# A first MoE layer with fp16 operand pairs, TensorE in order of emission, and attention over 14 of 16 chunks

## The chip, the core and the metric

The program runs on one core of one Trainium2 chip. The metric is the device time of one execution in microseconds (us), of which the median of several executions counts.

## The reference, cut to what matters

Attention over 4 batches, 8 heads, 576 positions and 64 columns a head (causal mask, and a bias that falls with the running sum of `max(s, 0)`), then two MoE layers of 2304 tokens, 512 model columns and 2048 features:

```python
attn = softmax(scores)                       # scores from q, k, the mask and cumsum(max(s, 0))
x = (attn @ v) as (2304 tokens, 512)
h = x @ w_in;  g = h * tanh(log1p(exp(h)));       x = g @ w_out      # first MoE
h = x @ w_in2; g = h / (1 + exp(-1.702 * h));     out = g @ w_out2   # second MoE
```

q, k, v and s come as float32, the four weights as float64.

## The kernel before, in words

**Numbers in pairs.** Nearly every product is made of operands that are split in a high and a low part, and of three matmuls: high by high, high by low, low by high (`mm3`, L814). In the first layer of the first MoE the parts are of type fp32r (32 bits), in the second MoE of fp16. The float64 weights are read as pairs of 32-bit words and joined on the chip: a Prelu on ScalarE, a shift and an or on VectorE; then a copy on ScalarE gives the high part and a subtraction on GpSimd the low part (`turn_w` L764; written apart as `turn_words`, `turn_join`, `turn_parts` at L793 to L812 for the first five weights).

**The stages.** (1) A prologue whose order is written out by hand (L868 to L944, mode "strict": each engine takes its instructions in the order of the program text). It loads, does the first six steps of attention, turns the first five of the 16 blocks of `w_in` and multiplies dummies (`warm`). (2) From there to the end of attention, `first_layer` (L968) makes h = x @ w_in for the first seven of nine spans of U = 256 tokens, in 16 chunks a span (one block of 128 features, 12 matmuls each). After every chunk `slot_a` (L962) runs as many attention steps (`tick`, L678) as the span owes. A tick emits the scores of step t (`do_qk`), their minimum on VectorE (`do_max`), the exponential on ScalarE (`do_exp`), the split in fp16 parts and their transposing DMA (`do_hilo`), the preparation of later groups of heads (`pop_prep`), and the product with v of the step LAG ticks back (`do_av`, `emit_tile`). Batch 0 has 26 steps of another form: its probabilities are transposed by TensorE and copied out by VectorE (`early_pt`), and its steps lag by 2. The other 78 steps use the DMA. (3) The last two spans (L1073 to L1088, 384 matmuls into accumulators named acc), while the 16 blocks of `w_out` are turned. (4) The second layer of the first MoE, and (5) the second MoE, both to the end of the program.

**What sets the order.** A scheduler with its own estimate of time orders each engine's instructions when the program is built. `Line` and `Lane` (L56 to L89) tie instructions to the one before: "strict" in the prologue; "after" from there to step 26, the first of batch 1 (NEAR), where an instruction is only kept behind the prologue's last; no tie from step 26 on (L690).

**Weights and buffers.** Twelve raw blocks of `w_in` are asked for at the start, on SyncE's queue (UP); a further one is asked for after a turned block (`bg_a`, L834). The pool wa has 16 buffers of 4 KB a partition, for raw blocks and for turned ones. The chunks' results go through the pool mo_a (MA = 5 buffers) to DRAM, written by SyncE's queue, and so do the loads of v for its scale (`vscale_load`, L312). Transposing DMAs stand on SyncE's queue too.

Of the kernel before, what the change touches and what calls it, by code (L numbers as in the profile page):

```python
# [18 lines left out]
PSC = 32768.0  # L19
VTOP = 16384.0  # L20
PH = 3
# [4 lines left out]
MA = 5  # L26
MBB = 2
# [4 lines left out]
HLB = 3  # L32
PB = 2
XTB = 2
PTB = 5
WAH = 3
NP0 = 5
FROM = 7
# [5 lines left out]
UQ = 2  # L44
WTOP = 8192.0
# [6 lines left out]
LAG = 4  # L52


class Line:
# [4 lines left out]
    def __init__(self, nc, tie):  # L60
        self.nc, self.tie, self.mode, self.last = nc, tie, None, {}
# [7 lines left out]
class Lane:  # L69
# [3 lines left out]
    def __getattr__(self, op):  # L73
# [4 lines left out]
        def run(*a, **kw):  # L78
# [14 lines left out]
def attention_moe_moe_kernel(  # L93
# [81 lines left out]


# [131 lines left out]

    vsc, vmx = {}, {}
# [14 lines left out]
    def vscale_set(b):  # L324
# [11 lines left out]
        nc.vector.tensor_scalar(out=t[:, 1:2], in0=t[:, 0:1], scalar1=PSC, scalar2=None, op0=ALU.mult)  # L336
# [273 lines left out]
    def norm_tile(x):  # L610
# [4 lines left out]
        nc.vector.tensor_scalar(out=rs, in0=su, scalar1=1e-9, scalar2=vsc[x["b"]][:, 1:2], op0=ALU.add, op1=ALU.mult)  # L615
        nc.vector.reciprocal(rs, rs)
        nc.gpsimd.tensor_tensor(out=ts["x"], in0=ts["x"], in1=rs.to_broadcast([128, nu, D]), op=ALU.mult)

    def emit_tile(x):
        b, i, n = x["b"], x["i"], x["n"]  # L620
# [6 lines left out]
        pv = ps[:, 0:KC * n].rearrange("p (c t) -> p c t", c=KC)  # L627
        t0 = b * S + 128 * i
        done = 0
        while done < n:  # L630
            u, off = divmod(t0 + done, U)
            m = min(n - done, U - off)
            if u not in xunit:
                xunit[u] = xh_a.tile([128, 2, KC, U], F32R, tag="xh", name="xh")
# [3 lines left out]
            nc.scalar.activation(out=hi, in_=src, func=AF.Copy)  # L638
            nc.vector.tensor_tensor(out=xu[:, 1, :, off:off + m], in0=src, in1=hi, op=ALU.subtract)
# [10 lines left out]
    def queue_prep(gi):  # L650
# [13 lines left out]
        items = items + vs  # L664
        if b + 1 < B and (i, g) in VSTEP:
# [14 lines left out]
    def tick():  # L680
        t = nxt[0]
        nxt[0] += 1
        if t < NS:
# [6 lines left out]
            if t >= NEAR:  # L690
                nc.mode = None
# [41 lines left out]
    I32 = mybir.dt.int32  # L733
# [30 lines left out]
    def turn_w(pool, lay, m, kind):  # L764
        t = pool.tile([128, 2, DM], F32R, tag="w", name="w")
        (win_t if kind == "in" else wout_t)[lay, m] = t
        r = fetched.pop((lay, m, kind))
        th, tl_ = t[:, 0, :], t[:, 1, :]
        if not wide:
            nc.scalar.activation(out=th, in_=r, func=AF.Copy)  # L770
            nc.vector.tensor_tensor(out=tl_, in0=r, in1=th, op=ALU.subtract)
            return
# [699 lines left out]
```

## Time and profile before

| what | us |
|---|---|
| three executions | 999.42, 1004.05, 1008.64 |
| median | 1004.05 |
| the profiled execution | 1001.29 |
| its span, first to last instruction | 999.3 |

The profile is of one execution: 2.0 us of its 1001.29 lie outside the span. PE is TensorE's matmuls, PEld its loading of weights, DVE VectorE, ACT ScalarE, POOL GpSimd, SP SyncE (SPq: a queue's own entries). All instructions carry line L79, that of the helper that records them, so they are told apart by the names of what they write and read: h<-xh,w is the first layer in its first seven spans, acc<-xh,w in its last two, h<-x,w2i the first layer of the second MoE, wst a raw block of weights, pt the transposed probabilities.

### The profile page before, as it was taken

The numbers are of one execution on the slowest core, as the hardware profiler recorded it, in microseconds if no ns is written. First come the engines' busy times: TensorE is split into PE (matmuls) and PEld (weight loads), VectorE is DVE, ScalarE is ACT, GpSimd is POOL, SyncE is SP. The second block draws the span as 40 slices with busy tenths as digits, with TensorE's granted clock in tenths as the row PEclk, the third lists the DMA queues.
The fourth block names the chain that finished last, engine by engine and source line by source line (L and its number), as shares of the span: only waits on it lengthen the run. The fifth ranks groups of instructions, "written<-read, shape, count | busy, mean of one in ns | idle before, by whom it ended". The sixth has DMA issues, their size and how long they took to land.

```text
span 999.3 us, 20234 instructions
## 1 busy us (share of the span) xinstructions
PE 968.8 (97%) x7974; PEld 863.0 (86%) x7974; DVE 676.8 (68%) x1363; ACT 554.3 (55%) x1062; POOL 289.1 (29%) x358
## 2 busy tenths in 40 slices
PE   8989998989999999999999999999999999999997
PEld 6868996979889889998888888888888888888886
DVE  6878677774666874788997967985554654653553
ACT  5656577785667874786565845643333433333331
POOL 5636442442144330000000000054342424333341
PEclk9999999999999999999999999999999999999999
DMA  9931688996689977899995653400100100000000
GB/s 257 342 88 40 186 192 166 178 239 149 157 167 223 191 144 188 308 330 357 380 308 181 233 187 107 127 1 16 49 22 1 44 23 1 22 22 1 22 13 32
DMA packets 157262, 142.26 MB, mean 142 GB/s; under 512 B 90000, under 2 KB 126352, under 8 KB 157168
## 3 DMA queue, kind: packets, MB, share of 16 engines
q1 hardware_dynamic: 150240, 122.22, 43.9%
q0 software_dynamic: 6928, 18.75, 6.9%
q8 instruction: 63, 1.03, 0.4%
q14 instruction: 31, 0.25, 0.1%
HBM read 89.09 MB, written 32.58 MB: 122 GB/s over the span
## 4 chain that ended last, share of the span: by engine, by line
PE 83%; DMA 5%; DVE 4%; issue 2%; ACT 1%; POOL 0%; SPq 0%; DVEq 0%; POOLq 0%; ACTq 0%
PE h L79 31%; PE acc L79 25%; PE p L79 16%; PE s L79 5%; PE o L79 3%; DMA pt<-hl 3%; PE kt L79 1%; PE qt L79 1%; DMA qraw<-in_q_dram 1%; PE pt L79 1%; DMA vraw<-in_v_dram 1%; DVE w2l L79 1%; PE xt L79 0%; DVE P L79 0%; DMA vl<-in_v_dram 0%
## 5 line engine op out<-in xcount | busy, mean ns | idle before, releaser
L79 PE MATMUL h<-x,w2i 128*128 128x256 f16 x1728 | 199.8, 273 | 0.9 <-DVE z L79 0.9
L79 PE MATMUL h<-xh,w 128*128 128x256 f32 x1344 | 189.7, 290 | 1.7 <-POOL w L79 0.9
L79 PEld LDWEIGHTS <-w2i 128*128 128x128 f16 x1728 | 169.0, 98 | 20.7 <-issue 1.1
L79 PE MATMUL acc<-gh,w 128*128 128x512 f32 (+1 forms) x640 | 181.7, 369 | 0.0
L79 PEld LDWEIGHTS h<-xh,w 128*128 128x128 f32 x1344 | 169.1, 192 | 4.1 <-ACT w L79 1.5
L79 PE MATMUL p<-w2h,gl 128*128 128x256 f16 x504 | 136.1, 273 | 0.5 <-DVE gl L79 0.5
L79 PE MATMUL p<-w2l,gh 128*128 128x256 f16 x504 | 136.1, 273 | 0.0
L79 PEld LDWEIGHTS acc<-gh,w 128*128 128x128 f32 x640 | 116.1, 189 | 20.6
L79 PE MATMUL p<-w2h,gh 128*128 128x256 f16 x504 | 133.5, 273 | 0.2 <-DVE e L79 0.2
L79 PE MATMUL acc<-gl,w 128*128 128x512 f32 (+1 forms) x320 | 117.9, 368 | 0.0
L79 POOL TENSOR_TENSOR s<-z 128x256 f32<-128x256 f32 x72 | 54.8, 783 | 216.9 <-DVE z L79 213.3
L79 DVE TENSOR_TENSOR gl<-z,gh 128x1024 fp32r<-128x1024 f32 (+1 forms) x72 | 94.4, 1313 | 26.8 <-ACT gh L79 26.1
L79 ACT ACTIVATE sg<-h,spx 128x512 f32<-128x512 f32 x72 | 49.0, 680 | 110.5 <-PE h L79 110.5
L79 PEld LDWEIGHTS <-gh 128*128 128x128 f16 x1008 | 98.6, 98 | 11.7 <-issue 0.3
L79 DVE SCALAR_TENSOR_TENSOR z<-h,sg 128x512 f32<-128x512 f32 x72 | 49.5, 687 | 72.3 <-ACT sg L79 72.3
L79 ACT ACTIVATE P<-P,mx 128x384 f32<-128x384 f32 (+4 forms) x128 | 76.5, 599 | 34.8 <-DVE mx L79 33.1
L79 DVE TENSOR_TENSOR gl<-s,gh 128x1024 f16<-128x1024 f32 x36 | 44.3, 1232 | 64.3 <-ACT gh L79 64.3
L79 DVE CUSTOM_DVE_ANT_0 P<-s,ck 128x384 f32<-128x384 f32 (+4 forms) x128 | 61.6, 497 | 34.2 <-PE s L79 26.8
L79 ACT ACTIVATE gh<-z 128x1024 fp32r<-128x1024 f32 (+1 forms) x72 | 67.9, 947 | 28.5 <-DVE z L79 25.4
L79 ACT ACTIVATE gh<-s 128x1024 f16<-128x1024 f32 x36 | 38.0, 1057 | 81.3 <-POOL s L79 81.3
L79 PE MATMUL s<-kw,qw 128*128 128x288 f32 (+4 forms) x352 | 78.5, 333 | 3.1 <-DVE mx L79 1.8
L79 DVE SCALAR_TENSOR_TENSOR wst<-wst 128x512 int32<-128x512 int32 x96 | 70.9, 755 | 2.8 <-ACT wst L79 2.5
(146 smaller groups left out, 1635.1 us busy)
## 6 DMA issues: line engine op xcount, KB each, us to landing
h_d<-hs SPq DMA_DIRECT2D x36, 512.0 KB, 4.6
hg<-h_d SPq DMA_DIRECT2D x36, 512.0 KB, 6.2
wst<-in_moe_w_in_dram SPq DMA_DIRECT2D x32, 512.0 KB, 7.2
wst<-in_moe_w_out_dram SPq DMA_DIRECT2D x32, 512.0 KB, 6.1
x_d<-x SPq DMA_DIRECT2D x18, 256.0 KB, 3.4
out_dram<-o SPq DMA_DIRECT2D x9, 512.0 KB, 2.8
kraw<-in_k_dram POOLq DMA_DIRECT2D x32, 128.0 KB, 4.7
w_d<-w2y SPq DMA_DIRECT2D x16, 256.0 KB, 5.1
```

The lines of the kernel that those rows point to most:

```text
L79: r = f(*a, **kw)
```

## The change

**fp16 pairs.** A block of `w_in` is no longer turned alone but in pairs of blocks, in parts that the emission spreads out: `pair_words` and `pair_join` (as before), `pair_sum` (an Abs with its sum over the row, on ScalarE), `pair_col` (a small copy), `pair_scale` (a matmul with ones that adds the sums over the rows, then five small VectorE operations that make a power of two of them), `pair_parts` (high parts on ScalarE with that scale, the low part of one block on VectorE, that of the other by two operations on GpSimd). The pair's four parts take one buffer of wa in place of two. After each pair one more raw block is asked for. The x of batch 0 gets scales too, from the largest v (`v_peak`, ten reductions; `x_scale`, three times); for the other batches v is already scaled, and that scale is now kept in x (`norm_tile` multiplies by a constant in its place). The scales are taken out when a chunk's result is copied from PSUM (`evict`): a span that lies in two batches (three of the nine) takes two copies in place of one.

**TensorE's order.** From step 26 to the end of attention each TensorE instruction is tied to the one emitted before it; the other engines stay free.

**Attention over 14 chunks.** A span's ticks are spread over its first 14 chunks (EARLY = 2). LAG grows from 4 to 5.

**Buffers.** mo_a goes from 5 to 2, mo_b from 2 to 5; hl (the fp16 parts) from 3 to 4, pt from 5 to 7. The chunks' results, the loads of v for its scale and the last raw block use wa.

**The prologue** turns pairs 0 and 1 (four blocks in place of five), in another order.

```diff
-MA = 5
-MBB = 2
+MA = 2
+MBB = 5
-HLB = 3
+HLB = 4
-PTB = 5
+PTB = 7
+EARLY = 2
-LAG = 4
+LAG = 5
...
-            if i is not None and line.mode:
+            if i is not None and (line.mode or (line.pe and self.name == "tensor")):
                 if self.name in line.last:
                     line.tie(i, line.last[self.name])
-                if line.mode == "strict":
+                if line.mode == "strict" or (line.pe and self.name == "tensor"):
                     line.last[self.name] = i
...
+    def to_scale(t, src, tiny, top):
+        nc.vector.tensor_scalar(out=t, in0=src, scalar1=tiny, scalar2=1.0 / top, op0=ALU.max, op1=ALU.mult)
+        nc.vector.reciprocal(t, t)
+        pow2(t)
+
+    def over_rows(cols, n):
+        ps = ps_s.tile([128, 512], F32, tag="s", name="bd")
+        nc.tensor.matmul(out=ps[:, 0:n], lhsT=ones, rhs=cols, start=True, stop=True, skip_group_check=True)
+        return ps[:, 0:n]
...
+    def x_scale(k, ni):
+        t = sm_p.tile([128, 2], F32, tag="sx", name="sx", bufs=3)
+        ps = over_rows(vm0[:, 0:2 * ni], 2 * ni)
+        nc.vector.tensor_reduce(out=t[:, 0:1], in_=ps, axis=mybir.AxisListType.X, op=ALU.max)
+        to_scale(t[:, 0:1], t[:, 0:1], 1.0e-30, VTOP)
+        ev_table(k, t)
...
-            t = tmp_pair(F32, "vl")[:, 0:VW]
+            t = wa_p.tile([128, 1024], F32, tag="w", name="vl")[:, 0:VW]
...
-                xunit[u] = xh_a.tile([128, 2, KC, U], F32R, tag="xh", name="xh")
+                xunit[u] = xh_a.tile([128, 2, KC, U], F16, tag="xh", name="xh")
...
             if t >= NEAR:
-                nc.mode = None
+                nc.mode, nc.pe = None, True
...
+    def pair_sum(p):
+        wsm[p] = ws = sm_p.tile([128, 2], F32, tag="wsm", name="wsm")
+        for e in range(2):
+            r = fetched[0, 2 * p + e, "in"]
+            y, junk = (r[:, :, 1 - k].bitcast(F32) for k in range(2)) if wide else (r, tmp_pair(F32, "junk")[:, 0:DM])
+            fetched[0, 2 * p + e, "in"] = y
+            lut(junk, y, AF.Abs, accum_out=ws[:, e:e + 1])
...
+    def pair_scale(p):
+        ps = over_rows(wmx.pop(p), 2)
+        wkp[p] = k = sm_p.tile([128, 2], F32, tag="wk", name="wk")
+        k = k[:, 0:1]
+        nc.vector.tensor_reduce(out=k, in_=ps, axis=mybir.AxisListType.X, op=ALU.max)
+        to_scale(k, k, TINY, WTOP1)
+        nc.vector.reciprocal(isw[:, p:p + 1], k)
+
+    def pair_parts(p):
+        k = wkp.pop(p)[:, 0:1]
+        win_t[p] = t = wa_p.tile([128, 2, 2, DM], F16, tag="w", name="w")
+        for e in range(2):
+            y = fetched.pop((0, 2 * p + e, "in"))
+            hi, lo = t[:, e, 0, :], t[:, e, 1, :]
+            nc.scalar.activation(out=hi, in_=y, func=AF.Copy, scale=k)
+            if e:
+                nc.gpsimd.tensor_scalar(out=y, in0=y, scalar1=k, scalar2=None, op0=ALU.mult)
+                nc.gpsimd.tensor_tensor(out=lo, in0=y, in1=hi, op=ALU.subtract)
+            else:
+                nc.vector.scalar_tensor_tensor(out=lo, in0=y, scalar=k, in1=hi, op0=ALU.mult, op1=ALU.subtract)
+        fetch_a()
...
     def slot_a():
         done[0] += 1
-        while done[1] < todo[0] * done[0] // NF and attn_left():
+        while done[1] < min(todo[0], todo[0] * done[0] // (NF - EARLY)) and attn_left():
             tick()
             done[1] += 1
 
+    def evict(o, ps, p, t0, t1, n):
+        ov, pv = (x.rearrange("p (d t) -> p d t", d=n) for x in (o, ps))
+        for a, z, k in x_class(t0, t1):
+            e = ev_need(k)[:, p:p + 1]
+            if k == "u0":
+                nc.vector.tensor_tensor(out=e, in0=isw[:, p:p + 1], in1=sx[k][:, 1:2], op=ALU.mult)
+            nc.scalar.activation(
+                out=ov[:, :, a - t0:z - t0], in_=pv[:, :, a - t0:z - t0], func=AF.Copy, scale=e
+            )
...
-            t = tmp_pair(F32, "hs")
+            t = wa_p.tile([128, 1024], F32, tag="w", name="hs")
...
-                    while wq and (0, min(NF - 1, m + 2 * e + d + WAH)) not in win_t:
-                        bg_a()
+                    p = (m + 2 * e) // 2
+                    pairs_to(p + 4 + d, p + 2 + d)
                     l1_mm(ps[:, d * U:(d + 1) * U], 0, m + 2 * e + d, xr, d == 0)
                     each()
                 o = t[:, e * 512:(e + 1) * 512]
-                nc.scalar.activation(out=o, in_=ps, func=AF.Copy)
+                evict(o, ps, m // 2 + e, u * U, (u + 1) * U, 2)
```

## Rows read from the trace of the kernel before

**Rows 1.** The page: span and busy time of TensorE.
```profile
span 999.3 us, 20234 instructions
PE 968.8 (97%) x7974; PEld 863.0 (86%) x7974; DVE 676.8 (68%) x1363; ACT 554.3 (55%) x1062; POOL 289.1 (29%) x358
```

**Rows 2.** Busy us by stage: stretch, PE, PEld, DVE, ACT, POOL, clock, DMA share.
```profile
0.00:36.00 36.00, 30.95 (x221) 25.22 (x222) 23.87 (x51) 18.02 (x53) 15.22 (x29) 0.95 0.99 284
36.00:100.00 64.00, 58.08 (x454) 51.09 (x454) 53.87 (x114) 43.11 (x100) 37.15 (x42) 1.00 0.40 124
100.00:392.00 292.00, 279.84 (x2711) 255.69 (x2709) 203.04 (x561) 207.39 (x526) 101.98 (x138) 0.99 0.84 178
392.00:441.00 49.00, 49.00 (x399) 48.37 (x397) 34.53 (x59) 35.00 (x55) 0.61 (x1) 1.00 0.90 308
441.00:999.30 558.30, 550.90 (x4198) 482.62 (x4196) 361.54 (x581) 250.73 (x332) 134.18 (x149) 1.00 0.29 102
```

**Rows 3.** Groups by form, matmuls and weight loads: count, busy us, mean ns, idle before.
```profile
L79 PE MATMUL h<-x,w2i 128*128 128x256 f16 x1728 | 199.8, 273 | 0.9 <-DVE z L79 0.9
L79 PE MATMUL h<-xh,w 128*128 128x256 f32 x1344 | 189.7, 290 | 1.7 <-POOL w L79 0.9 <-ACT w L79 0.8
...
L79 PE MATMUL acc<-xh,w 128*128 128x256 f32 x384 | 46.9, 284 | 0.0
...
L79 PEld LDWEIGHTS h<-xh,w 128*128 128x128 f32 x1344 | 169.1, 192 | 4.1 <-ACT w L79 1.5 <-POOL w L79 1.1 <-DVE xh L79 0.2
L79 PEld LDWEIGHTS <-w2i 128*128 128x128 f16 x1728 | 169.0, 98 | 20.7 <-issue 1.1
```

**Rows 4.** Timeline of PE (start, us, what): two chunks of the second MoE.
```profile
677.20 2.78 PE L79 MATMUL h<-x,w2i 128*128 128x256 f16 x24
679.82 0.27 PE L79 MATMUL p<-w2h,gh 128*128 128x256 f16 x1
```

**Rows 5.** Timeline of PE: a chunk of the first MoE.
```profile
326.26 1.68 PE L79 MATMUL h<-xh,w 128*128 128x256 f32 x12
327.77 0.40 PE L79 MATMUL s<-kw,qw 128*128 128x256 f32 x2
```

**Rows 6.** Busy us by stage, of the tile h alone: two stretches.
```profile
36.00:100.00 64.00, 25.68 (x182) 22.67 (x182) 0.00 (x0) 4.10 (x7) 1.00 0.40 124
100.00:392.00 292.00, 163.82 (x1162) 146.28 (x1162) 0.00 (x0) 28.76 (x49) 0.99 0.84 178
```

**Rows 7.** Busy us of all engines in one crowded stretch.
```profile
320.00:350.00 30.00, 28.21 (x287) 25.76 (x286) 26.34 (x66) 26.34 (x74) 12.23 (x17) 1.00 0.97 198
```

**Rows 8.** Groups of DVE by form, whole program: the join of a raw block.
```profile
L79 DVE SCALAR_TENSOR_TENSOR wst<-wst 128x512 int32<-128x512 int32 x96 | 70.9, 755 | 2.8 <-ACT wst L79 2.5
```

**Rows 9.** Groups of DVE by form, 0 to 105 us.
```profile
L79 DVE SCALAR_TENSOR_TENSOR wst<-wst 128x512 int32<-128x512 int32 x16 | 17.2, 1101 | 0.5 <-ACT wst L79 0.5
...
L79 DVE TENSOR_SCALAR wst<-wst 128x512 int32<-128x512 int32 x16 | 7.9, 522 | 2.3 <-DMA wst<-in_moe_w_in_dram 2.3
...
L79 DVE TENSOR_SCALAR vs<-vs 128x1 f32<-128x1 f32 x2 | 0.3, 144 | 0.0
...
L79 DVE TENSOR_REDUCE vs<-vx 128x1 f32<-128x128 f32 x1 | 0.3, 284 | 0.0
```

**Rows 10.** Groups of ACT by form, 0 to 105 us.
```profile
L79 ACT ACTIVATE wst<-wst 128x512 f32<-128x512 f32 x16 | 10.4, 679 | 1.2 <-DMA wst<-in_moe_w_in_dram 1.2
...
L79 ACT ACTIVATION_READ_ACCUMULATOR P<-P,mx 128x1 f32 x17 | 3.2, 188 | 0.0
```

**Rows 11.** Timeline of POOL: three subtractions for raw blocks.
```profile
42.54 3.86 POOL L79 TENSOR_TENSOR w<-wst,w 128x512 fp32r<-128x512 f32 x3
```

**Rows 12.** Waits of PE, 100 to 392 us: total us, times, longest.
```profile
PE o L79 <- DMA pt<-hl: 7.1, 6, 2.7
```

**Rows 13.** DMA issues, 100 to 392 us: count, median us to landing.
```profile
pt<-hl SPq DMA_TRANSPOSE x78, 3.8
```

**Rows 14.** Timeline of DVE: six joins in a row, beside rows 11.
```profile
39.96 8.21 DVE L79 SCALAR_TENSOR_TENSOR wst<-wst 128x512 int32<-128x512 int32 x6
```

More of the change, by code (lines that the diff above doesn't have):

```diff
@@ L664, in queue_prep @@
         items = items + vs
+        if b == 0:
+            items = items + [lambda: v_peak(i, g)]
+            if g and i == 3:
+                items = items + [lambda: x_scale("u1", 4)]
+            if g and i == 4:
+                items = items + [lambda: x_scale("u2", 5)]
         if b + 1 < B and (i, g) in VSTEP:
@@ L762, in fetch_w, with to_f32 @@
         fetched[lay, m, kind] = r
[L764 to L772, printed above, removed]
+    def to_f32(r, first):
         zi, yi = r[:, :, 0], r[:, :, 1]
         y = yi.bitcast(F32)
-        sided = lay == 0 and kind == "in"
-        if sided:
+        if first:
             held(lut(y, y, AF.Prelu, scale=2.0 ** -112, alpha=-(2.0 ** 32)))
@@ L781, in turn_w @@
         nc.vector.scalar_tensor_tensor(
-            out=yi if sided else zi, in0=yi, scalar=3, in1=zi, op0=ALU.logical_shift_left, op1=ALU.bitwise_or
+            out=yi if first else zi, in0=yi, scalar=3, in1=zi, op0=ALU.logical_shift_left, op1=ALU.bitwise_or
         )
-        if not sided:
+        if not first:
             nc.vector.scalar_tensor_tensor(
@@ L827, in attention_moe_moe_kernel @@
     nxt = [0]
-    wq = list(range(NP0, NF))
+    wq = [0, 0]
     fq = list(range(NF))
@@ L833, in fetch_a, with pairs_to @@
             fetch_w(None, 0, fq.pop(0), "in")
-    def bg_a():
-        if wq:
-            m = wq.pop(0)
-            turn_w(wa_p, 0, m, "in")
-            if m >= FROM:
-                fetch_a()
+    def pairs_to(pa, pb):
+        for k, f, n in ((0, pair_a, pa), (1, pair_b, pb)):
+            while wq[k] < min(n, NF // 2):
+                if not k:
+                    f(wq[k])
+                    pair_col(wq[k])
+                else:
+                    f(wq[k])
+                wq[k] += 1
     pt_p = st_t.enter_context(tc.tile_pool(name="pt", bufs=PTB, reuse_waits="tile"))
@@ L874, in attention_moe_moe_kernel @@
         v_load(i_, g, nc.sync)
-    for _ in range(UP):
+    while len(fq) > NF - UP:
         fetch_a()
@@ L892, in attention_moe_moe_kernel @@
     warm(12)
-    turn_words(0)
+    pair_words(0)
+    for g in range(2):
+        v_peak(0, g)
     score(2)
     early_turn(1, 1)
+    early_pt(steps[1])
+    pair_join(0)
+    early_av(steps[0])
+    score(3)
     load_group(0, 2, 0, False)
@@ L904, in attention_moe_moe_kernel @@
         )
-    early_pt(steps[1])
-    turn_join(0)
-    early_av(steps[0])
-    turn_parts(0)
-    turn_words(1)
-    score(3)
     early_pt(steps[2])
     early_av(steps[1])
-    turn_join(1)
-    turn_parts(1)
-    emit_tile(steps[1])
-    turn_words(2)
+    pair_sum(0)
+    for g in range(2):
+        v_peak(1, g)
+    emit_tile_turn(steps[1])
+    x_scale("u0", 2)
+    emit_tile_parts(steps[1])
     score(4)
+    pair_col(0)
     early_pt(steps[3])
     early_av(steps[2])
-    turn_join(2)
+    pair_scale(0)
+    pair_words(1)
     score(5)
-    turn_parts(2)
-    turn_words(3)
+    pair_parts(0)
+    pair_join(1)
     early_pt(steps[4])
```

150 lines of the change are left out of this document (104 added, 46 removed).

## The prediction

> **What bounds the kernel now.** I read the page's engine table first, then the busy time by stage, then the groups of matmuls, and last the waits. The table shows TensorE busy for 968.8 of 999.3 us [rows 1]; its idle 30.5 us are all that better overlap alone could give. The stages [rows 2] say where they lie: 5.0 us in the prologue (0 to 36), 5.9 us in batch 0 (36 to 100), 12.2 us in batches 1 to 3 (100 to 392), none in the last two spans (392 to 441), 7.4 us in all that follows. The reader is to see that from 441 on nothing is edited and TensorE sets the pace, so those 558 us stay; and that the first 441 us are of three kinds. In batches 1 to 3 TensorE has the largest share (280 of 292 us) but ScalarE and VectorE have 70% each and the DMA engines 84%. In batch 0 VectorE is at 53.9 of 64 us (84%) while TensorE waits more. The last two spans are TensorE alone.
>
> How much narrower operands can give is read from the groups [rows 3]. In the last two spans 384 matmuls of 32-bit parts take 46.9 us, 122 ns each, while the loads of their weights last 192 ns against 98 for fp16. The second MoE runs the same 128x256 shape in fp16: 24 of them start at 677.20 and the next group at 679.82 [rows 4], 2.62 us, 109 ns each.
>
> **The change part by part.**
>
> *fp16 in the last two spans.* 384 x (122 - 109) ns = 5.0 us, all on the path, as TensorE never waits there [rows 2]. Bounds 4 and 6.
>
> *fp16 in the first seven spans.* One chunk of 12 runs from 326.26 to 327.77 before the next work of TensorE starts [rows 5]: 1.51 us, against half of 2.62, 1.31. That is 0.20 us x 112 chunks = 22.4 us, the lower bound of TensorE's own time. The upper comes from the groups: 189.7 us / 1344 = 141 ns, against 199.8 / 1728 = 116 ns [rows 3], 25.5 ns x 1344 = 34.3 us, since a chunk that is cut into pieces pays at every cut. I take 26, nearer the row of one chunk. Of the 1344 matmuls 1162 lie after 100 us [rows 6], 86%: 22.5 us. The remaining 3.5 us fall in batch 0, where I count them at nothing: VectorE is ahead of TensorE there, and TensorE would only wait for longer. Not all of the 22.5 will show. From 320 to 350 us VectorE and ScalarE are busy for 26.3 of 30 us each [rows 7]; about 119 matmuls at 19 ns out of that stretch, 2.3 us, would put them at 95%. For such stretches I take off 4 us and keep 18.5; the ends are 0 (another resource holds the stage at its length) and 29.5 (86% of 34.3).
>
> *Making the weights.* Per pair VectorE gains one low part of 512 columns, at 0.76 to 1.10 us by the join of the same size [rows 8, 9], and some six tiny operations: a reduction like the 0.28 us row, the others like the 0.14 us row [rows 9]. About 0.9 + 1.0 = 1.9 us. ScalarE gains two Abs with their sums, 2 x (0.68 + 0.19) = 1.7 us [rows 10]. GpSimd keeps two operations a pair; its multiply has no row, and I take the 1.3 us of the subtraction (three in 3.86 us [rows 11]); bounds 0.6 and 2.6, hidden at 37 of 64 us busy [rows 2].
>
> In the prologue that is two pairs, four peaks of v at some 0.4 us (between the 0.28 us row and twice that) and one scale of x at 0.9, less the fifth block, which moves out (0.52 + 1.10 [rows 9]): VectorE +4.7 us, with 12.1 us free there [rows 2]. The order is written by hand, and two new matmuls wait in it for VectorE's small copy and, before it, for the Abs; behind each stand the transposes and products of batch 0's first steps. I put 2 us on the path (bounds 0 and 5).
>
> In batch 0 come six pairs (11.5 us), six peaks (2.4) and two scales (1.7): 15.6 us on a VectorE with 10.1 us free [rows 2]. If it packs fully, the stretch grows by 5.5 us; if it stays at 84%, by 18.6. I take 7, nearer the first, since the gaps that the rows show there are VectorE's own waits for chunks and scores, which the scheduler has more work to fill with. Start together: +9 us. Eleven added matmuls at some 0.1 us lie inside it.
>
> *TensorE in order of emission, LAG 5.* Removed: the scheduler's choice, by which a chunk is sometimes cut up; added: a wait of any one instruction now holds all of TensorE that is emitted behind it, the chunks too. Of the 12.2 idle us after 100 us, 7.1 are six waits for the transposing DMA, at most 2.7 us each [rows 12]. A tick lasts 292 / 78 = 3.7 us now and some 3.4 after; a lag of 5 gives the chain 17.2 us in place of 15.0, 2.2 us more, near the longest of these waits. More buffers of hl and pt keep its writers free. I count -4 us; the ends are -12 (all idle time) and +39, if each of 78 ticks stalled for half a microsecond, which a stage with 4% idle gives no sign of.
>
> *Attention over 14 chunks.* No work changes. The last two chunks of a span, 2.6 us, now cover the turning of the next span's x; on the other side ticks come 16/14 as dense, with the DMA at 84% already [rows 2]. Taken at 0, ends -3 and +4.
>
> *Copies and buffers.* The second copy of three spans adds 24 x about 0.2 us on ScalarE, spread over a stage where it has 85 us free. Results, loads of v and raw blocks share wa's 16 buffers; a load that waits for one stands on SyncE's queue ahead of the chunks' stores and the transposes, and then a product with v waits. At 0, with +3 as the other end; transposes land in 3.8 us [rows 13].
>
> *Sum.* 1001.3 - 5.0 - 18.5 + 9 - 4 = 982.8, called 983, made against the profiled execution (span 999.3 and 2.0 around it). That execution is 2.8 us under the median of 1004.05; the runs spread over 9 us, so I leave it. About 1% (10 us) is what a measurement of this kernel tells from no change.
>
> **The rivals.**
>
> *B, TensorE all the way.* Whole chunks in a fixed order take the upper price and the waits vanish: 1001.3 - 5.0 - 29.5 - 12 + 4 = 959. For it: TensorE's share of 96% after 100 us. Against: VectorE and ScalarE would go from 70% to 82%, the DMA from 84% to 98%.
>
> *C, the stage is held by its DMAs and its softmax.* TensorE's saved time turns into waits for pt and mx; the stage from 100 to 392 gives 6 us only, and the start costs its 9: 1001.3 - 5.0 - 6 + 9 = 999. For it: the DMA share of 0.97 at 320 to 350 [rows 7] and the six waits for pt. Against: TensorE is idle for 4% there.
>
> *D, the start is held by VectorE and GpSimd.* Six joins in a row took 8.21 us, 1.37 each [rows 14], while GpSimd subtracted [rows 11], against 0.76 on average [rows 8]. If the 20.3 us added in the first 100 us run at that rate, x 1.8, on an engine that stays busy for 84% of the time, they are 43.5 us, and the gains of 27.5 do not cover them: 1001.3 - 27.5 + 43.5 = 1017. It decides once the start grows by more than 27.5 us. The Trainium skill, page "SBUF — State Buffer", section "Who interferes with whom", states that VectorE and GpSimd share a pair of ports as an exclusive lock, and that a VectorE operation with two inputs in SBUF contends with GpSimd's reads; the added low part is of that kind, and by that rule D holds wherever the two meet. The trace agrees at 40 to 48 us (1.37 us) and not on average (0.76 us). Against D: GpSimd works 37 of 64 us in batch 0, descriptors included [rows 2], and all 16 joins of the first 105 us have a mean of 1.10 [rows 9].
>
> That the change does nothing of what it says is no rival: the operands' type is in the code, and both paces are rows.
>
> **How the numbers follow.** Forecast 52%, B 20%, C 17%, D 11%. The range 958 to 1003 leaves out D and a little of B; the forecast's own is 972 to 994. Faster by over 1% (below 994): all of the forecast but 1%, B, and 5 of C, 76%. Slower by over 1% (above 1014): D, 11%. Within: 13%.
>
> **What would show each step.** Right: the first layer's groups in f16 with some 116 ns of busy time per matmul and 98 ns loads; 16 matmuls of 12 back to back per span; about 42 us for the 384; the stage of batches 1 to 3 some 22 us shorter with 8 us idle; batch 0 and prologue some 9 us longer with VectorE over 90%. Wrong: first matmul of h later than 45 us or batch 1 later than 120 us (D); more than 20 us of waits for pt or mx after batch 1 begins (C); idle TensorE under 3 us there (B).

## The result, and the profile after

| | before | after |
|---|---|---|
| executions | 20 | 20 |
| median, us | 1003.94 | 1010.88 |
| lowest to highest, us | 999.42 to 1009.35 | 1007.40 to 1015.47 |
| the profiled execution: time, span, us | 1001.29, 999.3 | 1011.96, 1010.2 |

The ratio of the times is 1.0073, with a 95% interval of 1.0058 to 1.0088. The change costs 0.7%; the forecast was 983 us, and its range ended at 1003.

The page of the kernel after, against [rows 1]:

```profile
span 1010.2 us, 20395 instructions
...
PE 956.4 (95%) x7985; PEld 827.5 (82%) x7985; DVE 693.6 (69%) x1460; ACT 572.7 (57%) x1118; POOL 293.2 (29%) x360
```

TensorE is busy for 12.4 us less and the span is 10.9 us longer, so its idle time went from 30.5 to 53.8 us. The narrower operands did give time; something else took it twice over. The groups of TensorE by form, against [rows 3]:

```profile
L78 PE MATMUL h<-xh,w 128*128 128x256 f16 x1344 | 169.6, 279 | 6.9 <-ACT xh L78 2.1 <-ACT w L78 2.1 <-DVE xh L78 1.6
L78 PE MATMUL acc<-xh,w 128*128 128x256 f16 x384 | 42.1, 273 | 0.0
...
L78 PEld LDWEIGHTS <-w 128*128 128x128 f16 x1728 | 167.3, 100 | 30.0 <-issue 4.7 <-ACT w L78 2.3 <-DVE w L78 1.3
```

The two groups fell by 20.1 and 4.8 us. To see where the rest went, the span is cut where the same work begins: the first chunk of h, the first chunk of the second span, the first acc<-xh, the first acc<-gh. Busy time by stage (columns as in [rows 2]), the kernel after:

```profile
0.00:42.50 42.50, 33.94 (x224) 26.92 (x225) 26.86 (x72) 19.76 (x59) 13.77 (x29) 0.88 1.01 293
42.50:128.50 86.00, 71.18 (x594) 60.06 (x592) 73.81 (x215) 61.00 (x143) 50.05 (x54) 0.96 0.33 95
128.50:405.90 277.40, 254.57 (x2583) 217.87 (x2582) 199.00 (x542) 205.21 (x533) 94.46 (x128) 0.96 0.92 184
405.90:447.70 41.80, 41.80 (x386) 37.46 (x384) 34.41 (x58) 33.01 (x51) 0.00 (x0) 1.00 0.89 321
447.70:1010.20 562.50, 554.88 (x4210) 485.22 (x4207) 359.56 (x578) 253.77 (x335) 134.91 (x149) 1.00 0.28 101
```

The kernel before, cut at the same places:

```profile
0.00:35.80 35.80, 30.75 (x220) 25.05 (x220) 23.68 (x50) 17.82 (x53) 15.22 (x29) 0.95 0.99 284
35.80:113.10 77.30, 70.52 (x580) 62.36 (x578) 61.78 (x135) 48.61 (x112) 44.06 (x51) 1.00 0.46 136
...
113.10:392.00 278.90, 267.60 (x2588) 244.59 (x2584) 195.32 (x541) 202.09 (x513) 95.06 (x128) 0.99 0.84 178
392.00:438.70 46.70, 46.70 (x389) 46.45 (x387) 32.98 (x55) 33.26 (x53) 0.61 (x1) 1.00 0.90 310
```

| part | before | after | difference | forecast |
|---|---|---|---|---|
| prologue, to the first chunk of h | 35.8 | 42.5 | +6.7 | +2 |
| first span (most of batch 0) | 77.3 | 86.0 | +8.7 | +7 |
| spans 2 to 7, here "the stage" | 278.9 | 277.4 | -1.5 | -22.5 |
| last two spans | 46.7 | 41.8 | -4.9 | -5.0 |
| all that follows | 560.6 | 562.5 | +1.9 | 0 |
| span | 999.3 | 1010.2 | +10.9 | -18.5 |

The forecast was cut at 36, 100 and 392 us; each of its terms stands on the row that comes nearest. Two rows miss by more than 2 us. The stage gave 1.5 us instead of 22.5, and the start (the first two rows) took 15.4 instead of 9. In the stage TensorE was busy for 13.0 us less and idle for 22.8 us where it had been idle for 11.3. The clock that it was granted there is 0.96 in place of 0.99. What TensorE waited for in the stage after (total us, times, longest):

```profile
PE qt L78 <- ACT qraw L78: 9.7, 4, 5.2
PE o L78 <- DMA pt<-hl: 3.3, 4, 1.6
PE o L78 <- DVE x L78: 2.6, 3, 1.7
PE h L78 <- ACT xh L78: 2.1, 2, 1.3
PE h L78 <- DVE xh L78: 1.6, 2, 1.2
```

The waits of [rows 12], for pt, fell from 7.1 to 3.3 us. A wait took their place that the kernel before does not have at all: the turning of a later group's q (qt) waits for ScalarE to scale it (qraw). The longest of these in the timeline of PE after (in brackets: us of waiting, and for what):

```profile
220.33 1.48 PE L78 MATMUL h<-xh,w 128*128 128x256 f16 x12
221.57 0.48 PE L78 MATMUL s<-kw,qw 128*128 128x256 f32 x2
...
227.67 1.12 PE L78 MATMUL qt<-ident,qraw 128*128 128x128 f32 x4 [5.18 <-ACT qraw L78]
...
230.47 2.74 PE L78 MATMUL h<-xh,w 128*128 128x256 f16 x12
232.86 0.77 PE L78 MATMUL s<-kw,qw 128*128 128x256 f32 x2
```

And ScalarE's timeline over the same time:

```profile
223.10 0.42 ACT L78 ACTIVATE kraw<-kraw 128x256 f32<-128x256 f32 x1 [3.67 <-DMA kraw<-in_k_dram]
...
225.18 0.40 ACT L78 ACTIVATE P<-P,mx 128x128 f32<-128x128 f32 x1 [0.66 <-DVE mx L78]
...
227.21 0.40 ACT L78 ACTIVATE qraw<-qraw 128x256 f32<-128x256 f32 x1
```

This is read from the bottom up. q is scaled at 227.21, since ScalarE had first stood 3.67 us for a load of k and then done the work queued behind it. q is not urgent: its scores come ticks later. But qt stands in TensorE's fixed order ahead of a chunk of h, whose operands are long there, and the chunk stands still with it. The chunk at 220.33 needs 1.24 us to the next work, the one at 230.47 needs 2.39. The granted clock in three windows tells why (columns as before):

```profile
215.00:222.00 7.00, 7.00 (x86) 6.46 (x84) 4.54 (x17) 4.41 (x16) 4.00 (x5) 1.00 1.23 159
222.00:228.00 6.00, 0.82 (x7) 0.64 (x6) 3.12 (x13) 4.24 (x15) 0.00 (x0) 0.89 1.23 193
228.00:234.00 6.00, 6.00 (x46) 4.66 (x44) 2.91 (x9) 5.11 (x14) 2.97 (x4) 0.54 1.05 219
```

After the pause TensorE works without a gap at 0.54 of full speed, nearly the lower of its two levels (1.2 of 2.4 GHz); from 227.7 to 233.5 us it is 0.50. A pause is paid for twice: while it lasts, and in the matmuls behind it.

Step 26, from which the tie acts, is emitted behind the first chunk of the second span, so in the start the tie plays no part. There VectorE has 100 us of work in place of 85 (26.86 + 73.81 against 23.68 + 61.78), and the start is longer by just as much. Which of the new work does it could not be read from one trace.

### The profile page after: what moved, and what is told of

It is laid out like the page before. It is cut to its first block, busy times and chain, and to the rows that moved or that the text cites. A ratio compares the mean times of both kernels' runs of the same rounds, so it can differ in the third digit from the quotient of the medians.

```text
span 1010.2 us, 20395 instructions
## 1 busy us (share of the span) xinstructions
PE 956.4 (95%) x7985; PEld 827.5 (82%) x7985; DVE 693.6 (69%) x1460; ACT 572.7 (57%) x1118; POOL 293.2 (29%) x360
## 4 chain that ended last, share of the span: by engine, by line
PE 62%; DVE 2%; DMA 2%; ACT 1%; issue 1%; POOL 0%; SPq 0%; DVEq 0%; ACTq 0%; POOLq 0%
PE acc L78 24%; PE h L78 20%; PE p L78 16%; PE s L78 1%; DMA kraw<-in_k_dram 1%; DMA ck<-cum_d 1%; PE o L78 1%; DVE hl L78 0%; ACT P L78 0%; DMA vraw<-in_v_dram 0%; DMA pt<-hl 0%; DVE w2d L78 0%; DVE w2l L78 0%; PE xt L78 0%; ACT hl L78 0%
## 5 line engine op out<-in xcount | busy, mean ns | idle before, releaser
L78 PEld LDWEIGHTS <-w 128*128 128x128 f16 x1728 | 167.3, 100 | 30.0 <-issue 4.7
L78 PE MATMUL h<-xh,w 128*128 128x256 f16 x1344 | 169.6, 279 | 6.9 <-ACT xh L78 2.1
L78 DVE TENSOR_TENSOR gl<-z,gh 128x1024 fp32r<-128x1024 f32 (+1 forms) x72 | 93.5, 1302 | 31.7 <-ACT gh L78 30.5
L78 DVE TENSOR_TENSOR gl<-s,gh 128x1024 f16<-128x1024 f32 x36 | 44.1, 1225 | 66.6 <-ACT gh L78 66.6
L78 PE MATMUL s<-kw,qw 128*128 128x288 f32 (+4 forms) x352 | 82.3, 347 | 1.8 <-DVE p L78 1.0
L78 DVE CUSTOM_DVE_ANT_0 P<-s,ck 128x384 f32<-128x384 f32 (+4 forms) x128 | 61.4, 496 | 27.3 <-PE s L78 16.7
L78 POOL DMA_DIRECT2D x<-x_d x5 | 3.8, 767 | 239.4 <-DMA wst<-in_moe_w_in_dram 182.7
```

What stands on the lines that cost most here:

```text
L78: r = f(*a, **kw)
```

## The experiments

I held the fixed order of TensorE for the cause in the stage and the measured scales for the cause in the start. The rivals were that fp16 gives little in the stage whatever the order; that the 14 chunks crowd the ticks; and, in the start, that it is the low parts on GpSimd and VectorE. Each run is one edit, in e6_fixed_scale a bundle of edits, of the kernel before, of the kernel after, or of another run. This table gives all of them, with the times of the traces cut as above; idle is TensorE's, the length of the stage less its busy time. The last column is the median of 4 to 20 executions and its ratio to the kernel before, which ran beside each group of runs. Where the order is free, some attention (a last product with v, a last turning) slips past the end of the stage into the last two spans, so lengths are compared over both.

| run | start | its VectorE work | stage | TensorE busy, idle | last two spans | traced execution | median, ratio to before (95%) |
|---|---|---|---|---|---|---|---|
| before | 113.1 | 85.5 | 278.9 | 267.6, 11.3 | 46.7 | 1001.3 | 1003.9 |
| after | 128.5 | 100.7 | 277.4 | 254.6, 22.8 | 41.8 | 1012.0 | 1010.9, 1.0073 (1.0058 to 1.0088) |
| e1_no_order | 130.3 | 100.5 | 265.4 | 251.3, 14.1 | 44.2 | 1004.3 | 1004.1, 0.9999 (0.9975 to 1.0024) |
| e2_before_order | 111.9 | 85.6 | 296.5 | 272.6, 23.9 | 46.3 | 1017.1 | 1014.6, 1.0102 (1.0070 to 1.0133) |
| e3_sixteen | 131.5 | 101.9 | 274.6 | 250.7, 23.9 | 42.1 | 1011.0 | 1013.2, 1.0093 (1.0067 to 1.0119) |
| e5_fp16_only | 132.4 | 101.9 | 262.0 | 248.3, 13.7 | 47.3 | 1006.0 | 1004.0, 0.9995 (0.9971 to 1.0018) |
| e6_fixed_scale | 112.1 | 82.4 | 260.6 | 251.3, 9.3 | 44.2 | 981.5 | 987.7, 0.9828 (0.9778 to 0.9878) |
| e7_low_on_vector | 130.9 | 99.9 | 266.7 | 253.3, 13.4 | 44.2 | 1004.7 | 1000.8, 0.9953 (0.9921 to 0.9984) |
| e8_more_raw | 132.2 | 100.2 | 280.7 | 253.6, 27.1 | 41.8 | 1017.3 | 1014.0, 1.0100 (1.0057 to 1.0144) |
| e9_order_14 | 111.6 | 86.2 | 286.2 | 268.6, 17.6 | 46.1 | 1006.6 | 1006.4, 1.0023 (0.9997 to 1.0049) |
| e10_fixed_order | 116.1 | 82.1 | 275.9 | 254.3, 21.6 | 41.8 | 998.0 | 993.3, 0.9899 (0.9850 to 0.9948) |
| e11_x_measured | 120.3 | 90.4 | 261.9 | 251.0, 10.9 | 44.2 | 991.0 | 992.9, 0.9907 (0.9876 to 0.9939) |
| e12_scaled_copy | 127.7 | 95.4 | 270.4 | 254.5, 15.9 | 44.1 | 1005.2 | 1003.1, 0.9971 (0.9944 to 0.9999) |
| e13_fixed_16 | 115.5 | 84.1 | 268.8 | 253.1, 15.7 | 47.9 | 996.7 | 996.1, 0.9923 (0.9896 to 0.9950) |

A trace is one execution, and its time can lie some us off the median: that of e6_fixed_scale is the fastest of its four (981.5 against 987.7), that of e10_fixed_order the slowest of its four (998.0 against 993.3). How far two traces differ by chance is seen in the start, where pairs of runs that differ only behind it are 1.2 us (before, e2_before_order), 1.8 us (after, e1_no_order) and 4.0 us (e6_fixed_scale, e10_fixed_order) apart. So prices are given below from the traces, which show the place, and from the ratios, which show the size.

### The order taken out, and put in alone

**e1_no_order**: the kernel after with TensorE left to the scheduler.

```diff
-                nc.mode, nc.pe = None, True
+                nc.mode = None
```

> The changed kernel with the tie on TensorE's order taken out; all else stays. Theory O (the fixed order holds the stage: the 21 us that fp16 saves from the second span's first chunk to the last two spans go into engine-wide waits and into the lower granted clock after them): that stage falls from 277 us to 255-265, waits of TensorE in it from 23 to under 12 us, time near 995. Theory S (softmax engines and DMA supply the stage, in whatever order): it stays at 274-280 us and the waits move to pt and mx; time 1007-1013.

**e2_before_order**: the kernel before with the order alone (and the small change of `Line` and `Lane` that it needs).

```diff
-                nc.mode = None
+                nc.mode, nc.pe = None, True
```

> The kernel before with only the tie on TensorE's order from step 26 on. Theory O: TensorE gains waits of 5 us and more for the copies of q and k ahead of their transposes, the granted clock falls several times, and the time grows by 10-20 us to 1012-1024. Theory S: the order costs under 5 us, since the same engines supply the same work.

Busy time of the stage, e1_no_order:

```profile
130.30:395.70 265.40, 251.26 (x2562) 215.81 (x2561) 196.23 (x538) 205.04 (x531) 95.45 (x127) 0.97 0.90 188
```

The same of e2_before_order:

```profile
111.90:408.40 296.50, 272.63 (x2585) 250.65 (x2584) 196.87 (x542) 201.19 (x512) 95.23 (x129) 0.96 0.79 167
```

Without the order the stage is 12.0 us shorter: 8.7 us less idle time and 3.3 us less busy time for the same matmuls. The last two spans take 2.4 us more, so 9.6 us are won in all; by the ratios it is 7.4 us, 0.9999 for 1.0073. The whole kernel is then equal to the one before, and not near the 995 us that theory O expected, since the start is as long as in the kernel after. With the order alone the kernel before loses 17.6 us in the stage (12.6 idle, 5.0 busy), 17.2 over both; by the ratio 10.2 us. So the order costs, on either set of operands. What e2_before_order's TensorE waited for in the stage:

```profile
PE h L79 <- ACT xh L79: 9.6, 5, 3.4
PE o L79 <- DMA pt<-hl: 5.4, 6, 1.7
PE h L79 <- DVE xh L79: 3.2, 1, 3.2
```

These are other waits than those of the kernel after: the first chunk of a span waits for the turned x, since with 16 chunks the span's last tick stands right before it. It is the border that the 14 chunks were made for, which the next runs take up.

### 14 or 16 chunks

**e3_sixteen**: the kernel after with 16 chunks.

```diff
-EARLY = 2
+EARLY = 0
```

> The changed kernel with attention spread over all 16 chunks again (EARLY = 0). Theory E (the denser ticks starve TensorE): the stage falls by 5-10 us. Theory O: with the order fixed the last ticks of a span stand right ahead of the next span's chunks, which wait for x: the stage grows by 2-6 us (six borders of 1 us or less). Theory S: no change within 3 us.

**e5_fp16_only**: e1_no_order, with 16 chunks and the old lag: fp16 and the buffers alone.

```diff
-EARLY = 2
+EARLY = 0
-LAG = 5
+LAG = 4
```

> The changed kernel without the tie, without the 14 chunks and with LAG 4: fp16 pairs and buffers alone. Theory O: the stage is 255-265 us as without the tie alone, the start as late as in the changed kernel (second span at 126-130 us), time 993-1000. Theory S: the stage 274-280 us, time 1007-1013.

**e9_order_14**: e2_before_order with 14 chunks.

```diff
-        while done[1] < todo[0] * done[0] // NF and attn_left():
+        while done[1] < min(todo[0], todo[0] * done[0] // (NF - 2)) and attn_left():
```

> The kernel before with the tie on TensorE's order and attention over 14 of 16 chunks. Theory B (what the order costs the kernel before is TensorE's wait for x at the borders of spans, 14.2 us in its trace): waits for xh fall to under 4 us, the stage from 296 to 280-286 us, time 999-1005. Theory W: the waits move, and the stage stays above 290 us.

The waits of e3_sixteen in the stage are those of e2_before_order again:

```profile
PE h L78 <- ACT xh L78: 8.3, 5, 2.0
PE h L78 <- DVE xh L78: 3.3, 5, 1.1
```

On the kernel before, with the order, 14 chunks take 10.3 of the 17.6 us back (286.2 against 296.5), and the waits of h for xh shrink from 12.8 to 4.5 us, near what theory B had asked for. On the kernel after they remove the same waits (11.6 to 3.7 us), but the stage is 277.4 against 274.6: qraw takes their place, at 9.7 us against 1.8. The times of the two, 1010.9 and 1013.2, have intervals that overlap, and the stage differs by less than the 3 us that theory S of e3_sixteen allowed. On the kernel before the times are apart (1.0102 and 1.0023). So the 14 chunks mend one harm of the fixed order. Without the order, and with measured scales, they had nothing to mend: e1_no_order and e5_fp16_only, which differ by the chunks and by LAG, agree within 0.2 us of 1004. The rival that the ticks are crowded falls with the same pair.

e5_fp16_only is also the plainest measure of fp16 after the start: 16.9 us in the stage, less 0.6 in the last two spans, 16.3 over both (e1_no_order: 16.0). Its time of 1004.0 is not in the 993 to 1000 us of theory O, as its start ends at 132.4 us, later than the 126 to 130 expected.

### More raw buffers

**e8_more_raw**: the kernel after with one more buffer for qraw and one for kraw, so that the loads can be asked for earlier.

```diff
-bufs=2 if nm == "qraw" else 3
+bufs={"qraw": 3, "kraw": 4, "vraw": 3}[nm]
...
```

> The changed kernel, tie included, with one more buffer for the raw q tiles and one for the raw k tiles. Theory L (with the order fixed, TensorE waits for copies of q and k whose loads are issued too late, as the two or three buffers come free too late): the 15 us of waits of qt and kt for qraw and kraw fall to under 6, the stage falls from 277 to 265-270 us, time 999-1004. Theory W (the waits only move to the next late one, since every engine-wide stop takes the slack of the others): the stage stays above 272 us.

What its TensorE waited for in the stage:

```profile
PE o L78 <- DVE x L78: 5.7, 2, 5.2
PE o L78 <- DMA pt<-hl: 4.8, 5, 1.5
PE qt L78 <- ACT P L78: 4.6, 1, 4.6
PE kt L78 <- DVE qw L78: 3.9, 3, 2.0
PE xt L78 <- DVE mx L78: 3.0, 2, 2.6
```

The wait for qraw is gone and the time is not: five others share it, and the stage is no shorter (280.7), as theory W had it. So the named wait was not what held the stage. With e1_no_order this points to the order itself: any late operand, of any kind, stops the chunks behind it.

### The scales of the start

In four runs, e6, e10, e11 and e13, scales stand as constants, and the work of measuring them is left out: of the weights and of batch 0's x in three, of the weights alone in e11.

**e6_fixed_scale**: e1_no_order with constants for the scales. The Abs with its sums, the small copies, the matmuls with ones and the small VectorE operations go, and a low part is one GpSimd subtraction. The constant for the weights is taken into the scale of the Prelu that joins them. The new prologue and the shared buffers stay.

```diff
-            nc.scalar.activation(out=hi, in_=y, func=AF.Copy, scale=k)
-            if e:
-                nc.gpsimd.tensor_scalar(out=y, in0=y, scalar1=k, scalar2=None, op0=ALU.mult)
-                nc.gpsimd.tensor_tensor(out=lo, in0=y, in1=hi, op=ALU.subtract)
-            else:
-                nc.vector.scalar_tensor_tensor(out=lo, in0=y, scalar=k, in1=hi, op0=ALU.mult, op1=ALU.subtract)
+            nc.scalar.activation(out=hi, in_=y, func=AF.Copy)
+            nc.gpsimd.tensor_tensor(out=lo, in0=y, in1=hi, op=ALU.subtract)
...
+        nc.gpsimd.memset(t[:, 0:1], 2.0 ** 15)
+        nc.gpsimd.memset(t[:, 1:2], 2.0 ** -15)
...
+            nc.gpsimd.memset(isw, 2.0 ** -16)
```

> Without the tie on TensorE, and the scales of the weights and of batch 0's x are constants (2 to the 16 and 15): the Abs sums, the peaks of v and the matmuls and tiny operations that turn them into scales are left out, and the low parts go back to one subtraction each on GpSimd. fp16 stays. Theory V (the late start is the vector engine's added work): the second span starts at 112-118 us in place of 130, the stage behind it stays at 260-267 us, time 982-992. Theory R (the start is late through the new order of the prologue and the shared buffers): it starts at 124 or later and the time stays above 996.

**e11_x_measured**: e6_fixed_scale with `v_peak` and `x_scale` as in the kernel after.

```diff
-        nc.gpsimd.memset(t[:, 0:1], 2.0 ** 15)
...
+        ps = over_rows(vm0[:, 0:2 * ni], 2 * ni)
+        nc.vector.tensor_reduce(out=t[:, 0:1], in_=ps, axis=mybir.AxisListType.X, op=ALU.max)
+        to_scale(t[:, 0:1], t[:, 0:1], 1.0e-30, VTOP)
...
```

> Constant scales for the weights, but the scale of batch 0's x measured as in the changed kernel (ten peaks of v, three matmuls with ones and what follows). Theory V (the start is paid by vector work, and 5 us of 20 belong to x): the second span starts at 115-119 us, time 991-995. If the matmul and the tiny operations ahead of x are what delays (a chain and no load), it starts at 120 us or later, the first chunk at 38 us or later.

Busy time in the start and in the stage, e6_fixed_scale:

```profile
0.00:112.10 112.10, 97.52 (x798) 81.79 (x798) 82.43 (x199) 67.00 (x164) 56.42 (x89) 0.98 0.64 187
112.10:372.70 260.60, 251.28 (x2570) 215.24 (x2567) 198.34 (x544) 207.24 (x536) 96.39 (x128) 0.99 0.92 191
```

The start is back at 112.1 us, 18.2 less than in e1_no_order, and VectorE's work is 18.1 us less; the medians are 16.4 us apart. So the measured scales, with the low parts that came with them, are what made the start longer, and theory R falls, as the new prologue and buffers are still there. In e11_x_measured the scales of x bring back 8.2 us of the length and 8.0 of the work; the rest, 10.0 us, is that of the weights' scales and parts. With 4 us of chance between traces, x's share is 4 to 8 us. The stage of e6_fixed_scale is 4.8 us shorter too (TensorE idle for 9.3 us where e1_no_order has 14.1); its trace is 6.2 us under its median, so that this is a gain of the edits is not shown.

**e7_low_on_vector**: e1_no_order with both low parts on VectorE, none on GpSimd.

```diff
-            if e:
-                nc.gpsimd.tensor_scalar(out=y, in0=y, scalar1=k, scalar2=None, op0=ALU.mult)
-                nc.gpsimd.tensor_tensor(out=lo, in0=y, in1=hi, op=ALU.subtract)
-            else:
-                nc.vector.scalar_tensor_tensor(out=lo, in0=y, scalar=k, in1=hi, op0=ALU.mult, op1=ALU.subtract)
+            nc.vector.scalar_tensor_tensor(out=lo, in0=y, scalar=k, in1=hi, op0=ALU.mult, op1=ALU.subtract)
```

> Without the tie on TensorE, and the second block's low part too in one operation on VectorE, in place of two on GpSimd (2.2 and 1.2 us each). Theory V: VectorE gains 8 x 0.76 = 6 us, the second span starts 3-7 us later than 130 us. Theory G (GpSimd's multiply of 2 us is the slow link: it holds the parts, and the loads of q and k that GpSimd issues stand behind it): the second span starts 4-10 us earlier, at 120-126 us, and the time falls to 994-1000.

**e12_scaled_copy**: e1_no_order with a scaled copy on ScalarE in place of the multiplies, and one GpSimd subtraction for each low part.

```diff
...
+            nc.scalar.activation(out=y, in_=y, func=AF.Copy, scale=k)
+            nc.gpsimd.tensor_tensor(out=lo, in0=y, in1=hi, op=ALU.subtract)
```

The five lines that go are those of e7_low_on_vector.

> Without the tie, all scales measured, but the low parts made as before the change: ScalarE scales the block in place (0.68 us more per block), GpSimd subtracts once. VectorE loses 8 low parts (6 us), GpSimd 8 multiplies (16 us). Theory V: the second span starts 4-8 us earlier than 130 us, time 995-1000. If the chain of Abs, sum, matmul and scale is what delays, it starts at 128 us or later and the time stays at 1001-1006.

Neither moves the start by more than 2.6 us (130.9 and 127.7 against 130.3), which is inside what chance gives, so the low parts and GpSimd alone are not what made it longer by 15 us. In e7_low_on_vector neither theory came true. The groups of DVE by form up to 128 us, e7_low_on_vector:

```profile
L78 DVE SCALAR_TENSOR_TENSOR w<-wst,wk,w 128x512 f16<-128x512 f32 x16 | 11.9, 767 | 2.2 <-ACT w L78 2.2
L78 DVE SCALAR_TENSOR_TENSOR wst<-wst 128x512 int32<-128x512 int32 x16 | 10.3, 681 | 0.0
L78 DVE TENSOR_SCALAR wst<-wst 128x512 int32<-128x512 int32 x16 | 6.4, 435 | 4.7 <-DMA wst<-in_moe_w_in_dram 4.7
```

The same of the kernel after, up to 125 us, against [rows 9]:

```profile
L78 DVE SCALAR_TENSOR_TENSOR wst<-wst 128x512 int32<-128x512 int32 x16 | 11.4, 744 | 0.0
L78 DVE TENSOR_SCALAR wst<-wst 128x512 int32<-128x512 int32 x16 | 9.2, 617 | 3.8 <-DMA wst<-in_moe_w_in_dram 3.8
...
L78 DVE SCALAR_TENSOR_TENSOR w<-wst,wk,w 128x512 f16<-128x512 f32 x8 | 6.1, 760 | 1.8 <-ACT w L78 1.8
...
L78 DVE CAST wmx<-wsm 128x2 bf16<-128x2 f32 x8 | 2.1, 261 | 0.0
```

e7_low_on_vector gives VectorE eight more low parts, 5.8 us, and its sum does not rise, since joins and shifts take 16.7 us in place of 19.9 in e1_no_order (20.6 in the kernel after); that this comes from GpSimd's having less to do is not shown. Over all runs of the table the start is VectorE's work plus 25 to 34 us, with the work between 82 and 102. VectorE's free time hardly took up what was added: +15.2 us of work went with +15.4 us of start (before, after), 18.1 with 18.2 and 8.0 with 8.2, but the 5.2 us that e12_scaled_copy takes away with 2.6 only.

Whether that is because the new operations are links of the chain that the start waits for (Abs, small copy, matmul, power of two, high and low part, chunk) or because VectorE's gaps lie where nothing is ready, the runs don't tell apart. The marks set for the chain were just met by e11_x_measured (start 120.3 for "120 us or later", first chunk 38.2 for "38 us or later") and, but for 0.3 us of start, by e12_scaled_copy (127.7 and 1003.1). But e11_x_measured added 8 us of VectorE work where 5 had been counted on, and all of this is within the 4 us of chance.

### The order and the 16 chunks, with the start out of the way

**e10_fixed_order**: e6_fixed_scale with the order.

```diff
-                nc.mode = None
+                nc.mode, nc.pe = None, True
```

> The kernel with constant scales, now with the tie on TensorE's order. Theory O (the order is a cost of its own, as large whether the start is early or late): the stage from the second span to the last two grows from 261 to 270-275 us, time from 988 to 997-1003, waits there for x, q and k in place of pt. Theory I (the order hurt the changed kernel only because everything was late behind its start): the stage stays under 265 us and the time within 4 us of 988.

**e13_fixed_16**: e6_fixed_scale with 16 chunks and the old lag.

```diff
-EARLY = 2
+EARLY = 0
-LAG = 5
+LAG = 4
```

> Constant scales, no tie, and attention over all 16 chunks with LAG 4, as before the change. If 14 chunks and LAG 5 are worth anything without the tie, the time is 3 us and more over 988; if not (as between the two kernels without the tie and with measured scales, 1004.1 and 1004.0) it is within 3 us of it.

With the short start the order costs 15.3 us in the stage of these traces (12.3 idle, 3.0 busy), 12.9 over both parts. The two traces are the fastest and the slowest of their runs; the ratios, 0.9828 and 0.9899, give 7.1 us, and their intervals overlap a little. So theory I (nothing once the start is short) gets no support, and the 997 to 1003 us of theory O were not reached (993.3). The price of the order in all pairs:

| without and with the order | chunks | traces, stage and last two spans, us | ratios, in us |
|---|---|---|---|
| before, e2_before_order | 16 | 17.2 | 10.2 |
| e5_fp16_only, e3_sixteen (LAG 4 and 5) | 16 | 7.4 | 9.8 |
| e1_no_order, after | 14 | 9.6 | 7.4 |
| e6_fixed_scale, e10_fixed_order | 14 | 12.9 | 7.1 |
| before (16 chunks), e9_order_14 | 14 | 6.7 | 2.3 |

By the ratios it is about 10 us with 16 chunks and 2 to 7 with 14; the 2.3 of e9_order_14 can't be told from nothing.

The 14 chunks with LAG 5 are worth 8.4 us of the median behind the short start without the order (e6_fixed_scale against e13_fixed_16), while with measured scales they were worth nothing (1004.1 against 1004.0). The two traces are 15.3 us apart, of which 8.2 lie in the stage, 3.4 in the start and 3.7 in the last two spans. Why the chunks pay only behind a short start was not tried.

The fastest version is e6_fixed_scale, 0.9828 of the time before, for weights and values whose size is known. With x measured it is 0.9907. Among those that measure all scales e7_low_on_vector, at 0.9953, and e12_scaled_copy, at 0.9971, are the fastest, with intervals that overlap.

## Why the prediction was wrong

The forecast of the difference in span was -18.5 us and the measured one is +10.9. The 29.4 us between them are 21.1 from the stage and the last two spans (-6.4 where I had -27.5), the start's 6.4, and 1.9 elsewhere.

**The step that failed first: "TensorE in order of emission ... I count -4 us".** Measured by e1_no_order, which keeps LAG 5, it is +9.6 (12.0 in the stage, less 2.4 behind it), so 13.6 of the 21.1 us are here, and the sign is wrong; by the ratios it is +7.4. I had the mechanism in the text ("a wait of any one instruction now holds all of TensorE that is emitted behind it, the chunks too") and the end at +39, but then judged by the kernel before: "a stage with 4% idle gives no sign of" stalls. Those 4% were what was left with the scheduler free to put a chunk wherever an operand was late. They measured the cure and not the illness; the operands' lateness does not show in a trace in which something else always ran. The clock's share was no term of the sum at all. In the stage TensorE is busy for 1.0 to 5.0 us more with the order than without. There it stands at the lower clock for 20.5 us after and for 13.7 in e1_no_order (summed over stretches of 1 us of the traces); half of the difference, 3.4 us, is near the 3.3 us by which the two differ in busy time.

**The step that failed second: the prologue, "I put 2 us on the path (bounds 0 and 5)".** It is 6.7: 3.5 us of idle time, and 3.2 us that TensorE is busy for longer at a granted clock of 0.88 in place of 0.95. Timeline of PE after, ahead of the first chunk:

```profile
37.11 1.10 PE L78 MATMUL o<-v,p 128*128 128x64 f32 x8 [3.02 <-DVE x L78]
38.37 0.16 PE L78 MATMUL bd<-wmx,ones 128*128 128x2 bf16 x1 [0.16 <-DVE wmx L78]
...
42.47 1.25 PE L78 MATMUL h<-xh,w 128*128 128x256 f16 x10
```

The matmul that I suspected (bd) waits for 0.16 us. The product with v waits for 3.02 us, for a VectorE that has more to do before it: VectorE stands for 1.80 us until ScalarE's high part of a block is there, makes the low part at 33.68 us, and then has two joins and a copy ahead of the product's x. In e11_x_measured, with the scales of x, the first chunk is at 38.2 us, in e1_no_order at 43.6. With constants it is at 35.9, 36.9 and 38.5 us (e6, e13, e10), though no edit touches the prologue between these three. So the scales of the weights are what moved it; a share of x is not shown. Batch 0, "I take 7", is 8.7, inside its bounds of 5.5 and 18.6; VectorE, which was to be busy for over 90%, is at 86% (73.81 of 86.0 us). The work itself was sized well: 20.3 us estimated, 18.1 between e1_no_order and e6_fixed_scale; its cover was not there.

**A size: fp16 after the start, -18.5 and -5.0.** Without the order it is 16.0 to 16.3 us, so 7.2 to 7.5 of the 23.5 are missing, the rest of the 21.1. Over the stage and the last two spans TensorE is busy for 20.1 us less in e1_no_order than before, and idle for 4.1 us more. So the 4 us taken off for crowded stretches did come; the mis-sized term is the price of a chunk. I took 26 us for 112 chunks, 0.23 each; h is busy in the stage for 162.5 us before, 146.0 in e1_no_order and 144.0 after, 16.5 to 18.4 less for 96 chunks, 0.17 to 0.19 each and under my lower bound of 0.20. The idle time that came is C's mechanism at a small size: pt is waited for longer in e1_no_order, 10.3 us for the 7.1 of [rows 12].

**What was right.** The last two spans of the kernel after: 4.9 us for 5.0, with nothing of the attention left in them, and loads of 100 ns for 98. The busy time of one matmul of h fell from 141 to 126 ns, not to the 116 that I had named. The waits for pt are 2.4 to 4.8 us in the four runs with the order, LAG 5 and the larger pools, 5.4 and 8.5 in the two with the order and without these, which fits what LAG and the pools were to do, though no run takes them apart from the rest; with the order free it does not hold (10.3 in e1_no_order). 14 chunks: nothing either way with measured scales and a free order, which I had put at 0.

**The rivals.** B (TensorE all the way) asked for under 3 us of idle time; it is 22.8. C (DMA and softmax) asked for over 20 us of waits for pt or mx; pt has 3.3, and with the order gone the stage gets shorter under the same DMAs and softmax. D came nearest by its time, 1017, and its sign came true (the second span at 128.5 us, after the 120 named; 113.1 before), but by luck: the joins of the start were to run at 1.37 us and ran at 0.744, faster than the 1.10 of [rows 9], and the start grew by 15.4 us where D decides from 27.5. D's mechanism is real at a single join. DVE and POOL of the kernel before:

```profile
30.46 1.33 DVE L79 SCALAR_TENSOR_TENSOR wst<-wst 128x512 int32<-128x512 int32 x1 [0.53 <-ACT wst L79]
...
34.56 0.68 DVE L79 SCALAR_TENSOR_TENSOR wst<-wst 128x512 int32<-128x512 int32 x1
...
29.94 1.30 POOL L79 TENSOR_TENSOR w<-wst,w 128x512 fp32r<-128x512 f32 x1 [5.63 <-ACT w L79]
```

The join that meets a GpSimd subtraction takes 1.33 us, the other 0.68. The Trainium skill, page "SBUF — State Buffer", section "Who interferes with whom", states that a VectorE operation with two inputs in SBUF contends with a GpSimd operation that reads SBUF; these two joins agree. What D had wrong is how often the two meet: after the change only one group of four joins (at 45.45 us, 3.47 us) meets a subtraction. The sum over a start does not show the rule: the mean join is 681 ns in e7_low_on_vector and 684 in e6_fixed_scale, with GpSimd busy for 39 and 56 us.

## What to carry to other kernels

A trace taken under a free scheduler shows which waits were hidden and not how late the operands are; before an engine's order is fixed, look for every operand whose producer ends close before its use, on any engine, and price the fixed order by those, not by the idle time. Where one wait goes and the time stays, do not chase the next name on the list: run the kernel without the constraint that joins them. A price read from two traces holds the chance of two executions; set beside it the ratio of many. And work added to an engine with free time is free only if the free time lies at the place and off the chain; here nearly each us that VectorE gained in the start was a us of time.

## What the runs showed of the hardware that was not expected

A pause of TensorE of 5.2 us was followed by 6 us at a granted clock of 0.54, in which 12 matmuls took 2.39 us in place of 1.24. In the start, a wait of 5.7 us ends at 62.1 us, and the granted clock from there to 66 us is 0.50. Shorter waits came before such a fall too: 1.89 us ahead of 153.57 us, and 0.50 from 155 to 158 us. GpSimd's groups up to 125 us, after:

```profile
L78 POOL TENSOR_SCALAR wst<-wst,wk 128x512 f32<-128x512 f32 x8 | 15.8, 1974 | 40.3 <-DVE w L78 20.8 <-ACT w L78 17.9 <-issue 1.0
...
L78 POOL TENSOR_TENSOR w<-wst,w 128x512 f16<-128x512 f32 x8 | 10.2, 1275 | 0.4
```

The multiply with one input and a scale per row takes 1.97 us, more than the subtraction of two inputs, 1.28 (the shortest of each 1.62 and 1.15); I had taken them as equal. And VectorE's copy of two numbers a row to bf16 takes 0.16 us in the median and 0.75 us once, at 37.57 us: there it ends at 38.32, just behind a GpSimd subtraction that began at 37.13 and ends at 38.29. In the two runs without GpSimd's multiply, e7_low_on_vector and e12_scaled_copy, no copy takes more than 0.17 us.
